# An attention and SwiGLU decode block on one core: the last gate's weights loaded with the other modulation weights, w2 in four pieces, the last K and V in fewer transfers

## The chip, the cores and the metric

One core of a Trainium2 chip runs the kernel. The metric is the device time of one execution in microseconds; three runs of the kernel before gave 242.71, 242.87 and 242.71, median 242.71 us. A profiled execution, from which all rows below come, took 242.85 us.

## What is computed

A decode step of a transformer block for a batch of B = 4 tokens, D = 512, in float32. The vector `c` (4 x 512) goes through silu and `w_mod` (512 x 3072) and gives six modulations: sa, ca, ga for the attention half, sb, cb, gb for the feed-forward half.

```python
mod = (_silu(c) @ w_mod).reshape(c.shape[0], 6, 1, -1)
sa, ca, ga, sb, cb, gb = (mod[:, 0], mod[:, 1], mod[:, 2], mod[:, 3], mod[:, 4], mod[:, 5])
h = _layernorm(x, axis=-1) * (1 + ca) + sa
x = x + ga * _A_ref(h, A_k_cache, A_v_cache, A_wq, A_wo)
h = _layernorm(x, axis=-1) * (1 + cb) + sb
x = x + gb * _B_ref(h, B_w1, B_w3, B_w2)
return x
```

`_A_ref` is attention over the last 2048 cached positions, 32 query heads on 8 key-value heads, with the projections wq and wo. `_B_ref` is `(silu(h @ w1) * (h @ w3)) @ w2` with 1792 hidden columns.

## The kernel before

All weights and the used part of the caches are laid out on the host so that every load is one rectangle of 128 partitions. About 99 MB pass through SP's DMA queue, in the order in which `load` (L92 to L94) issues them.

**The attention.** The 8 key-value heads are taken in 4 pairs. A pair's even head lies in the buffer `KV[0]`, its odd head in `KV[1]`, 8192 columns of K and 8192 of V each (8 MB a head). `WP` holds wo of the pair in its first half and wq of the next pair in its second. PE runs the loop body `pair` (L331 to L358): `scores`, a transpose of the probabilities (`turn`), `values`, a transpose of the result, and for the pair's heads `proj_out` with wo into the bank `bA`. ACT does the exponentials and scalings, DVE maxima, sums and re-layouts. SP's loads wait for the matmuls that free a buffer (`x_done`, `a_done`, `qt_done`). POOL passes the landing of K and V of the odd head on to PE, as semaphores that PE counts down (L142 to L148).

**The last head.** wo of the last pair (2 MB), K (4 MB), the first three quarters of V (3 MB, `dva`) and the last quarter (1 MB, `dvb`) are four transfers (L118 to L121).

**The tail.** Behind the last head come `wm` (ga, sb, cb of w_mod, 3 MB), `f1` (w1 and a part of w3, 4 MB), `f2` (the rest of w3, 3 MB), `gw` (gb's part of w_mod, 1 MB, and the first 8 of 28 units of w2, 1 MB) and w2's other 20 units in five transfers that end at the units `W2_CUTS` names. A unit is 256 columns, 128 KB; each transfer has its own semaphore. The order in which PE takes them is written out by hand behind the loop ("post", from L391 on):

- the sum over the four row groups of the attention output (`a_sb`, then bM, L368), and silu(c) times `wm` in three column groups of PE (L395), which ACT copies out as ga, sb, cb (L402);
- x1 = x + ga * attention, its norm on DVE and ACT (`stats` L150, `rroot` L165), h turned to `h2T` (L421, L424);
- h times f1 in four column groups (L432 to L435), copied to `g_sb` and turned; h times f2 (L442 to L445), copied to `u_sb` and turned (L461, L464); silu of the gate times the up part, as `hidT` (L448 to L467);
- gb's product in four row blocks (L470 to L472), copied by ACT to `gb_sb` (L475) and later spread and copied again to `gbJ` (L498 to L500);
- w2: the first 16 units as eight wide matmuls of 512 columns into `bO` (L484 to L487); their sum over the row blocks is spread into `bX` by `spread` (L278) from `y_sb` (L496, L502). The other 12 units go straight into `bX` as matmuls of 64 columns, eight for two units (L488 to L492), over four column groups;
- y = x1 + gb * (h w2), with both in the same spread layout (L505, L507), and the store (L509).

A float32 matmul of the program stands as two records in the trace.

Of the kernel before, what the change touches and what calls it, by code (L numbers as in the profile page):

```python
# [11 lines left out]
P = 128  # L12
# [4 lines left out]
HEAD = 8  # L17

W2_CUTS = [0, 8, 16, 20, 24, 27, 28]
H = 64  # L20
PAIRS = G // 2
W2_AT = 8192
# [25 lines left out]
def block_kernel(nc, x_in, t0_in, t1_in, kv_in, w_in, wm_in, f1_in, f2_in, gw_in, w2_in, out):  # L48
# [15 lines left out]
    dx, dt0, dt1, dkv, dk, dva, dvb, dwo, dm, df1, df2 = sems("dx dt0 dt1 dkv dk dva dvb dwo dm df1 df2")  # L64
    dw = sems(" ".join(f"dw{i}" for i in range(len(W2_CUTS) - 1)))
    z_ok, q_ok, p_ok, k_ok, va_ok, vb_ok, pt_ok, o_ok, ot_ok = sems("z_ok q_ok p_ok k_ok va_ok vb_ok pt_ok o_ok ot_ok")
# [3 lines left out]
    KV = [sb("KV0", 16384), sb("KV1", 16384)]  # L70
    WP = sb("WP", 8192)
# [6 lines left out]
    q_sb, p_sb, o_sb, a_sb, y_sb, g_sb, u_sb, gb_sb = [sb(n, 512) for n in "q_sb p_sb o_sb a_sb y_sb g_sb u_sb gb_sb".split()]  # L78
# [3 lines left out]
    sa_sb, ga_sb, sb_sb, cb_sb = [sb(n, 512, B) for n in "sa_sb ga_sb sb_sb cb_sb".split()]  # L82
# [5 lines left out]
    zero = y_sb  # L88
# [8 lines left out]
    s.dma_start(WP[:, 4096:], t1_in).then_inc(dt1, 16)  # L97
# [4 lines left out]
    for p in range(PAIRS):  # L102
        if p == PAIRS - 1:
            break
        S.wait_ge(qt_done, 2 * p + 2)
        if p:
            S.wait_ge(a_done, 2 * p)
        if p < PAIRS - 2:
            load(WP, w_in[p], dwo)
        else:  # L110
            load(WP, w_in[p], dwo)
        S.wait_ge(x_done, 2 * p + 1)
        load(KV[0], kv_in[2 * p + 2], dkv)
        S.wait_ge(x_done, 2 * p + 2)
        if p < PAIRS - 2:
            load(KV[1], kv_in[2 * p + 3], dk)
    S.wait_ge(a_done, G - 2)
    load(WP[:, :4096], w_in[PAIRS - 1][:, :4096], dwo)  # L118
    load(KV[1][:, :8192], kv_in[G - 1][:, :8192], dk)
    load(KV[1][:, 8192:14336], kv_in[G - 1][:, 8192:14336], dva)  # L120
    load(KV[1][:, 14336:], kv_in[G - 1][:, 14336:], dvb)  # L121
    S.wait_ge(x_done, G - 1)
    load(KV[0][:, :6144], wm_in, dm)
    load(KV[0][:, 6144:14336], f1_in, df1)
    S.wait_ge(x_done, G)
    load(KV[1][:, :6144], f2_in, df2)
    load(KV[1][:, 6144:10240], gw_in, dw[0])
    for a, b, sem in zip(W2_CUTS[1:-1], W2_CUTS[2:], dw[1:]):
        load(KV[1][:, W2_AT + a * 256 : W2_AT + b * 256], w2_in[:, (a - 8) * 256 : (b - 8) * 256], sem)
# [12 lines left out]
    for p in range(PAIRS - 1):  # L142
        gp.wait_ge(dk, 16 * (p + 1))
        for sem in (k_ok, va_ok, vb_ok):
            gp.sem_inc(sem, 1)
    for d, sem, n in ((dk, k_ok, 16 * PAIRS), (dva, va_ok, 16), (dvb, vb_ok, 16)):
        gp.wait_ge(d, n)
        gp.sem_inc(sem, 1)  # L148
# [134 lines left out]
    def project(u):  # L283
        for k in range(4):
            at = 4096 + 2048 * u + 512 * k
            ins = mm(bQ[32 * k : 32 * k + B, :], hT[:, k * B : (k + 1) * B], WP[:, at : at + 512])
        ins.then_inc(q_done, 1)
# [16 lines left out]
    def proj_out(u):  # L304
        take(ot_ok)
        for r in range(R):
            at = 2048 * u + 512 * r
            ins = mm(bA[32 * r : 32 * r + B, :], oT[:, r * B : (r + 1) * B], WP[:, at : at + 512], False, True)
        ins.then_inc(a_done, 1)
# [22 lines left out]
    with nc.body("pair", parent=root, valid_engines=[ET.PE]):  # L332
        T.reg_add(reg, reg, 1)
        take(dkv, 16)
        take(z_ok)
        scores(KV[0])
        project(1)
        take(p_ok)
        turn(bP, p_sb, pp_done)
        take(q_ok)  # L340
        turn(bT, q_sb, qt_done)
        take(pt_ok)
        values(KV[0], {})
        take(o_ok)
        turn(bX, o_sb, x_done)
        take(k_ok)
        take(z_ok)
        scores(KV[1])
        take(p_ok)
        turn(bP, p_sb, pp_done)  # L350
        take(dwo, 16)
        proj_out(0)
        take(pt_ok)
        values(KV[1], {0: va_ok, 3: vb_ok})
        take(o_ok)
        turn(bX, o_sb, x_done)
        proj_out(1)
        T.br_lt(reg, PAIRS, on_true="query", on_false="leave")  # L358
# [37 lines left out]
    for k in range(4):  # L396
        for i in range(3):
            at = (3 * k + i) * 512
            ins = mm(bX[32 * i : 32 * i + B, :], sc[:, k * B : (k + 1) * B], KV[0][:, at : at + 512], k == 0, k == 3)
    ins.then_inc(pe, 1)  # L400
    A.wait((pe, 4))
    t_ga, t_sb, t_cb = [A.op(s.copy(dst, bX[32 * i : 32 * i + B, :])) for i, dst in enumerate((ga_sb, sb_sb, cb_sb))]  # L402
# [14 lines left out]
    t_x1J = A.op(s.copy(x1J, bS[:, :H]))  # L417

# [4 lines left out]
    V.wait((pe, 6))  # L423
# [8 lines left out]
    for k in range(4):  # L432
        for j in range(4):
            at = 6144 + k * 2048 + j * 512
            ins = mm(bQ[32 * j : 32 * j + B, :], h2T[:, k * B : (k + 1) * B], KV[0][:, at : at + 512], k == 0, k == 3)  # L435
    ins.then_inc(pe, 1)
    A.wait((pe, 7))
# [9 lines left out]
    A.wait((pe, 8))  # L447
# [12 lines left out]
    V.wait((pe, 9))  # L460
# [5 lines left out]
    V.wait((pe, 10))  # L466
    t_hid = V.op(v.tensor_mul(hv[:, :, :3], view(sT)[:, :, :3], view(bS)[:, :, :3, :B]))  # L467


    T.wait_ge(dw[0], 16)  # L470
    for k in range(4):
        ins = mm(bM[32 * k : 32 * k + B, :], sc[:, k * B : (k + 1) * B], KV[1][:, 6144 + 512 * k : 6144 + 512 * (k + 1)])  # L472
    ins.then_inc(pe, 1)
    A.wait((pe, 11))
    t_gb = A.op(s.copy(gb_sb, bM))  # L475
    T.wait_ge(V.sem, t_hid[1])
    for i in range(len(W2_CUTS) - 1):
        if i:
            T.wait_ge(dw[i], 16)
        for n in range(W2_CUTS[i], W2_CUTS[i + 1]):  # L480
            if n < 26 and n % 2:
                continue
            jj, c = CHUNKS[n // 2]
            if n < 2 * HEAD:  # L484
                at, k = W2_AT + n * 256, n // 2
                ins = mm(bO[32 * (k % 4) : 32 * (k % 4) + B, :], hv[:, c, jj, :], KV[1][:, at : at + 512], k < 4, k >= HEAD - 4)
                continue  # L487
            for j in range(4):  # L488
                for r in (n % 2,) if n >= 26 else (0, 1):
                    at = W2_AT + (n * 256 + j * H if n >= 26 else n * 256 + j * P + r * H)  # L490
                    w = half(hw[:, c, jj, :], r)
                    ins = mm(bX[32 * j : 32 * j + 32, :H], w, KV[1][:, at : at + H], False, n == 27)  # L492
        if i == 1:
            ins.then_inc(pe, 1)
            V.wait((pe, 12))
            t_y = V.op(v.tensor_copy(y_sb, bO))  # L496
            T.wait_ge(A.sem, t_gb[1])
            spread(bT, same, gb_sb)  # L498
            A.wait((pe, 13))
            t_gb = A.op(s.copy(gbJ, bT[:, :H]))  # L500
            T.wait_ge(V.sem, t_y[1])
            spread(bX, same, y_sb, True, False)  # L502
    ins.then_inc(pe, 1)
    V.wait((pe, 14), t_gb)
# [9 lines left out]
def _layout(i):  # L514
    import numpy as np

    def a(t):
        return np.ascontiguousarray(t)

    k = i["A_k_cache"][:, :, SK - W :, :].reshape(B, G, NT, 512, DH)  # L520
    v = i["A_v_cache"][:, :, SK - W :, :].reshape(B, G, NT, 4, P, DH)
    k = k.transpose(1, 4, 2, 0, 3).reshape(G, P, 8192)
    v = v.transpose(1, 4, 2, 0, 3, 5).reshape(G, P, 8192)
    wm = i["w_mod"].reshape(4, P, 6, 512).transpose(1, 0, 2, 3)
    c = i["c"].reshape(B, 4, P).transpose(2, 1, 0).reshape(P, 16)
    wq = i["A_wq"].reshape(4, P, G, 512).transpose(2, 1, 0, 3).reshape(G, P, 2048)
    wo = i["A_wo"].reshape(G, R, P, D).transpose(0, 2, 1, 3).reshape(G, P, 2048)
    pairs = [[wo[2 * p], wo[2 * p + 1]] + ([wq[2 * p + 2], wq[2 * p + 3]] if p < 3 else [wo[6], wo[7]]) for p in range(4)]
    w1 = i["B_w1"].reshape(4, P, FF).transpose(1, 0, 2)
    w3 = i["B_w3"].reshape(4, P, FF).transpose(1, 0, 2)  # L530
    w2 = i["B_w2"].reshape(14, P, D)
    w2 = np.stack([w2[4 * j + c_] for j, c_ in CHUNKS], 1)
    w2[:, 13] = w2[:, 13].reshape(P, 4, 2, H).transpose(0, 2, 1, 3).reshape(P, D)
    w2 = w2.reshape(P, 14 * D)
    return {
        "x_in": a(i["A_x"].reshape(B, D)),
        "t0_in": np.concatenate([c, wm[:, :, 1::-1].reshape(P, 4096)], 1),
        "t1_in": np.concatenate([wq[0], wq[1]], 1),
        "kv_in": np.concatenate([k, v], 2),
        "w_in": np.stack([np.concatenate(p, 1) for p in pairs]),  # L540
        "wm_in": a(wm[:, :, 2:5]).reshape(P, 6144),
        "f1_in": np.concatenate([w1, w3[:, :, 1536:]], 2).reshape(P, 8192),
        "f2_in": a(w3[:, :, :1536]).reshape(P, 6144),
        "gw_in": np.concatenate([a(wm[:, :, 5]).reshape(P, 2048), w2[:, : 4 * D]], 1),
        "w2_in": a(w2[:, 4 * D :]),
    }
# [22 lines left out]
```

## Time and profile before

| | us |
|---|---|
| median of three runs | 242.71 |
| profiled execution, whole | 242.85 |
| its span, first to last instruction | 241.5 |
| DMA queue of SP: share of 16 engines' span | 95.6% (99.13 MB) |
| PE busy (matmuls) | 135.7 (56%) |
| DVE busy | 38.5 (16%) |
| ACT busy | 24.2 (10%) |

The span is the program's own time; 1.35 us of the profiled execution lie around it. A busy PE is no PE at its peak, since matmuls are pipelined and their ends are modelled; PEclk is the granted share of TensorE's clock, 1.00 for 2.4 GHz and 0.50 for 1.2 GHz. The landing of a DMA is its issue time plus the time to landing. Where a view merges several instructions, it gives the first one's start and the stretch to the end of the last one.

### The profile page before, as it was taken

Reading aid. Unit: us, or ns where it says so; the run is one execution under the profiler, and the core shown is the slowest. Engines: PE = TensorE matmul, PEld = TensorE weight load, DVE = VectorE, ACT = ScalarE, POOL = GpSimd, SP = SyncE. Lnnn points to the kernel's source line nnn. Section 1 sums busy time; section 2 is a strip of 40 time slices with the busy share of each in tenths; the row PEclk is TensorE's granted clock in tenths of the full one; section 3 lists DMA queues with packets and bytes.
Section 4 is the critical chain, followed back from the end, with each engine's and each line's share of the span. In section 5 each row is a group of like instructions: output and inputs, shape, how many; then the busy total and the mean of one; then the engine's idle time right before and its main releaser. Section 6 shows DMA issues by size and latency. Waiting matters only on the chain. (4 is left out here: it accounts for less than half of the span.)

```text
span 241.5 us, 2424 instructions
## 1 busy us (share of the span) xinstructions
PE 135.7 (56%) x1020; PEld 39.1 (16%) x1020; DVE 38.5 (16%) x126; ACT 24.2 (10%) x51; POOL 2.3 (1%) x15
## 2 busy tenths in 40 slices
PE   3004547818773378176613871757228767674885
PEld 0000121301221012012100120112001222111213
DVE  3003202201200022012000220220002222115121
ACT  2002101100110021001200021011000201122100
POOL 3000000000000000000000000000000000000000
PEclk9999958976589599679965699779957997995899
DMA  7998989899989898999898989998989999999992
GB/s 272 446 501 358 510 361 499 369 423 429 516 358 510 358 510 360 429 434 505 369 499 369 499 369 423 434 510 369 499 347 440 436 406 444 452 431 396 431 400 105
DMA packets 3756, 101.30 MB, mean 419 GB/s; under 512 B 548, under 2 KB 676, under 8 KB 1064
## 3 DMA queue, kind: packets, MB, share of 16 engines
q1 hardware_dynamic: 3600, 99.13, 95.6%
q10 hardware_dynamic: 152, 2.11, 2.1%
q8 instruction: 3, 0.05, 0.1%
q14 instruction: 1, 0.01, 0.0%
HBM read 101.20 MB, written 0.03 MB: 419 GB/s over the span
## 5 line engine op out<-in xcount | busy, mean ns | idle before, releaser
L257 PE MATMUL bS<-KV,Z 128*16 128x512 f32 x256 | 42.7, 827 | 41.1 <-PEq L273 41.1
L257 PE MATMUL bO<-KV,pT 128*16 128x512 f32 x256 | 32.9, 658 | 0.5
L257 PEld LDWEIGHTS bS<-KV,Z 128*16 128x16 f32 x256 | 9.2, 123 | 69.1 <-issue 69.1
L220 DVE TENSOR_REDUCE MX<-bS 128x1 f32<-128x512 f32 x8 | 5.5, 692 | 82.2 <-PE bS L257 82.2
L382 ACT ACTIVATE p_sb<-bS,NB 128x512 f32<-128x512 f32 x8 | 5.5, 687 | 103.7 <-ACTq L373 103.7
L291 PE MATMUL bP<-ident,p_sb 128*128 128x128 f32 x32 | 5.5, 298 | 17.3 <-PEq L273 17.3
L257 PE MATMUL bM<-KV,sc 128*4 128x512 f32 x24 | 5.9, 711 | 16.0 <-DVE sc L190 16.0
L257 PE MATMUL bA<-WP,oT 128*4 128x512 f32 x64 | 10.4, 731 | 4.0 <-PEq L273 4.0
L257 PEld LDWEIGHTS bO<-KV,pT 128*16 128x16 f32 x256 | 8.4, 106 | 23.5 <-issue 23.5
L387 ACT ACTIVATE o_sb<-bO,LB 128x512 f32<-128x512 f32 x8 | 5.5, 687 | 48.9 <-ACTq L373 48.9
L291 PE MATMUL bX<-ident,o_sb 128*128 128x128 f32 x32 | 5.0, 280 | 7.8 <-PEq L273 7.8
L246 DVE TENSOR_REDUCE oT<-bX 128x16 f32<-128x64 f32 x8 | 1.8, 224 | 43.7 <-PE bX L291 43.7
L257 PE MATMUL bQ<-WP,hT 128*4 128x512 f32 x64 | 8.3, 592 | 0.6 <-DVE hT L199 0.6
L291 PEld LDWEIGHTS bP<-ident,p_sb 128*128 128x128 f32 x32 | 3.6, 150 | 24.4 <-issue 24.4
L291 PE MATMUL bT<-ident,q_sb 128*128 128x128 f32 x32 | 5.4, 296 | 3.6 <-PEq L273 3.6
L291 PEld LDWEIGHTS bX<-ident,o_sb 128*128 128x128 f32 x32 | 3.4, 140 | 15.0 <-issue 15.0
L229 DVE COPY pT<-bP 128x256 f32<-128x256 f32 x8 | 3.4, 425 | 14.1 <-PE bP L291 14.1
L257 PE MATMUL bQ<-KV,h2T 128*4 128x512 f32 x32 | 5.4, 842 | 0.3 <-DVE h2T L424 0.3
L291 PEld LDWEIGHTS bT<-ident,q_sb 128*128 128x128 f32 x32 | 3.6, 147 | 7.5 <-issue 7.2
L257 PE MATMUL bX<-KV,sc 128*4 128x512 f32 x24 | 4.4, 592 | 0.0
L257 PEld LDWEIGHTS bM<-KV,sc 128*4 128x4 f32 x24 | 0.9, 96 | 20.9 <-DVE sc L190 17.6
L204 DVE TENSOR_REDUCE Z<-bT 128x16 f32<-128x64 f32 x8 | 1.8, 225 | 14.5 <-PE bT L291 14.2
(104 smaller groups left out, 69.2 us busy)
## 6 DMA issues: line engine op xcount, KB each, us to landing
WP<-w_in SPq DMA_DIRECT2D x3, 4096.0 KB, 19.7
KV<-kv_in SPq DMA_DIRECT2D x1, 4096.0 KB, 24.0
KV<-f_in SPq DMA_DIRECT2D x1, 4096.0 KB, 25.6
KV<-kv_in SPq DMA_DIRECT2D x1, 3072.0 KB, 30.8
KV<-wm_in SPq DMA_DIRECT2D x1, 3072.0 KB, 16.3
KV<-f_in SPq DMA_DIRECT2D x1, 3072.0 KB, 18.8
KV<-t_in SPq DMA_DIRECT2D x1, 2056.0 KB, 12.3
WP<-t_in ACTq DMA_DIRECT2D x1, 2048.0 KB, 12.5
```

Source lines behind the costliest of these rows:

```text
L204: v.tensor_reduce(Z.rearrange("p (b i) -> p b i", b=B)[:, :, 12 : 12 + R], bT.rearrange("p (r k i) -> p i r k", r=R, k=4)[:, :B], axis=AX. ...
L220: t = V.op(v.reduce_max(MX[:, 0:1], bS, axis=AX.X))
L229: v.tensor_copy(pT.rearrange("p (t b c r) -> p c b t r", t=NT, b=B, c=4), bP.rearrange("p (c b i) -> p c b i", c=4, b=B)[:, :, :, :16].rea ...
L246: V.op(v.tensor_reduce(oT.rearrange("p (r b) -> p r b", r=R), diag, axis=AX.X, op=ALU.add), ot_ok)
L257: return T.matmul(o, lhsT, rhs, start=start, stop=stop, skip_group_check=True)
L291: ins = T.transpose(dst[:, c * P : (c + 1) * P], src[:, c * P : (c + 1) * P], ident)
L382: A.op(s.activation(p_sb, bS, AF.Exp, bias=NB[:, 0:1], accum_out=SM[:, 0:1]), p_ok)
L387: A.op(s.mul(o_sb, bO, LB[:, 0:1]), o_ok)
```

## The change

Three things change, and the buffers with them.

1. **gb's weights** move from the transfer `gw` behind f2 into `wm`, which has now four of w_mod's parts (4 MB) and goes into the first half of `KV[0]`, with f1 in the second half. gb's product is a fourth column group of the modulation matmuls; ACT copies it behind cb, and its spread into the layout of the result stands right behind x1's.
2. **w2** comes in four transfers of 16, 8, 3 and 1 units behind f2, and all 28 units run as matmuls of 64 columns straight into `bX`. The wide matmuls, `y_sb` and its spread are gone.
3. **The last head**: WP and `KV[1]` become two parts of one buffer, `WK`, with wq in WP's first half and wo in its second, beside K. So wo of the last pair and the last K are one transfer (6 MB) on the semaphore of K; POOL, when it lands, also releases PE's wait for wo. V of the last head is one transfer (4 MB).

```diff
-W2_CUTS = [0, 8, 16, 20, 24, 27, 28]
+W2_CUTS = [0, 16, 24, 27, 28]
...
-    KV = [sb("KV0", 16384), sb("KV1", 16384)]
-    WP = sb("WP", 8192)
+    WK = sb("WK", 8192 + 16384)
+    KV = [sb("KV0", 16384), WK[:, 8192:]]
+    WP = WK[:, :8192]
...
     S.wait_ge(a_done, G - 2)
-    load(WP[:, :4096], w_in[PAIRS - 1][:, :4096], dwo)
-    load(KV[1][:, :8192], kv_in[G - 1][:, :8192], dk)
-    load(KV[1][:, 8192:14336], kv_in[G - 1][:, 8192:14336], dva)
-    load(KV[1][:, 14336:], kv_in[G - 1][:, 14336:], dvb)
+    load(WK[:, 4096:16384], wk_in, dk)
+    load(KV[1][:, 8192:], v_in, dv)
     S.wait_ge(x_done, G - 1)
-    load(KV[0][:, :6144], wm_in, dm)
-    load(KV[0][:, 6144:14336], f1_in, df1)
+    load(KV[0][:, :8192], wm_in, dm)
+    load(KV[0][:, 8192:], f1_in, df1)
     S.wait_ge(x_done, G)
     load(KV[1][:, :6144], f2_in, df2)
-    load(KV[1][:, 6144:10240], gw_in, dw[0])
-    for a, b, sem in zip(W2_CUTS[1:-1], W2_CUTS[2:], dw[1:]):
-        load(KV[1][:, W2_AT + a * 256 : W2_AT + b * 256], w2_in[:, (a - 8) * 256 : (b - 8) * 256], sem)
+    for a, b, sem in zip(W2_CUTS[:-1], W2_CUTS[1:], dw):
+        load(KV[1][:, W2_AT + a * 256 : W2_AT + b * 256], w2_in[:, a * 256 : b * 256], sem)
...
-        for sem in (k_ok, va_ok, vb_ok):
+        for sem in (k_ok, v_ok):
             gp.sem_inc(sem, 1)
-    for d, sem, n in ((dk, k_ok, 16 * PAIRS), (dva, va_ok, 16), (dvb, vb_ok, 16)):
-        gp.wait_ge(d, n)
-        gp.sem_inc(sem, 1)
+    gp.wait_ge(dk, 16 * PAIRS)
+    gp.sem_inc(k_ok, 1)
+    gp.sem_inc(dwo, 16)
+    gp.wait_ge(dv, 16)
+    gp.sem_inc(v_ok, 1)
...
-        values(KV[1], {0: va_ok, 3: vb_ok})
+        values(KV[1], {0: v_ok})
...
-        for i in range(3):
-            at = (3 * k + i) * 512
+        for i in range(4):
+            at = (4 * k + i) * 512
...
-    t_ga, t_sb, t_cb = [A.op(s.copy(dst, bX[32 * i : 32 * i + B, :])) for i, dst in enumerate((ga_sb, sb_sb, cb_sb))]
+    t_ga, t_sb, t_cb, t_gb = [A.op(s.copy(dst, bX[32 * i : 32 * i + B, :])) for i, dst in enumerate((ga_sb, sb_sb, cb_sb, gb_sb))]
...
+    T.wait_ge(A.sem, t_gb[1])
+    spread(bO, same[:B], gb_sb)
+    A.wait((pe, 6))
+    t_gbJ = A.op(s.copy(gbJ, bO[:, :H]))
...
-    T.wait_ge(dw[0], 16)
-    for k in range(4):
-        ins = mm(bM[32 * k : 32 * k + B, :], sc[:, k * B : (k + 1) * B], KV[1][:, 6144 + 512 * k : 6144 + 512 * (k + 1)])
-    ins.then_inc(pe, 1)
-    A.wait((pe, 11))
-    t_gb = A.op(s.copy(gb_sb, bM))
     T.wait_ge(V.sem, t_hid[1])
     for i in range(len(W2_CUTS) - 1):
-        if i:
-            T.wait_ge(dw[i], 16)
+        T.wait_ge(dw[i], 16)
...
-            if n < 2 * HEAD:
-                at, k = W2_AT + n * 256, n // 2
-                ins = mm(bO[32 * (k % 4) : 32 * (k % 4) + B, :], hv[:, c, jj, :], KV[1][:, at : at + 512], k < 4, k >= HEAD - 4)
-                continue
...
-                    ins = mm(bX[32 * j : 32 * j + 32, :H], w, KV[1][:, at : at + H], False, n == 27)
-        if i == 1:
-            ins.then_inc(pe, 1)
-            V.wait((pe, 12))
-            t_y = V.op(v.tensor_copy(y_sb, bO))
-            T.wait_ge(A.sem, t_gb[1])
-            spread(bT, same, gb_sb)
-            A.wait((pe, 13))
-            t_gb = A.op(s.copy(gbJ, bT[:, :H]))
-            T.wait_ge(V.sem, t_y[1])
-            spread(bX, same, y_sb, True, False)
+                    ins = mm(bX[32 * j : 32 * j + 32, :H], w, KV[1][:, at : at + H], n == 0 and r == 0, n == 27)
```

The order of PE's instructions in the tail, from the product with f2 on, with the semaphores they wait for (`dw0` and on are the landings of w2's transfers in turn, `dve` and `act` those engines). Before:

```order
L257 MATMUL bA<-KV,h2T 4x512 [waits df2]
L464 MATMUL bS<-ident,u_sb 128x96 [waits dve]
L257 MATMUL bM<-KV,sc 4x512 [waits dw0]
L257 MATMUL bO<-KV,hidT 4x512 [waits dve]
L257 MATMUL bO<-KV,hidT 4x512 [waits dw1]
L257 MATMUL bT<-gb_sb,same 32x64 [waits act]
L257 MATMUL bX<-y_sb,same 32x64 [waits dve]
L257 MATMUL bX<-KV,hidT 32x64 [waits dw2]
L257 MATMUL bX<-KV,hidT 32x64 [waits dw3]
L257 MATMUL bX<-KV,hidT 32x64 [waits dw4]
L257 MATMUL bX<-KV,hidT 32x64 [waits dw5]
```

And in the changed kernel:

```order
L253 MATMUL bA<-WK,h2T 4x512 [waits df2]
L464 MATMUL bS<-ident,u_sb 128x96 [waits dve]
L253 MATMUL bX<-WK,hidT 32x64 [waits dw0,dve]
L253 MATMUL bX<-WK,hidT 32x64 x63
L253 MATMUL bX<-WK,hidT 32x64 [waits dw1]
L253 MATMUL bX<-WK,hidT 32x64 x31
L253 MATMUL bX<-WK,hidT 32x64 [waits dw2]
L253 MATMUL bX<-WK,hidT 32x64 x11
L253 MATMUL bX<-WK,hidT 32x64 [waits dw3]
```

gb's product and spread and the wide part of w2 have left this stretch; behind `hidT` stand 112 small matmuls (64, 32, 12 and 4) with four waits.

The order of SP's loads from the last pair's wo on, before:

```order
L94 DMA WP<-w_in 128x4096 [waits a_done,x_done]
L94 DMA KV<-kv_in 128x8192
L94 DMA KV<-kv_in 128x6144
L94 DMA KV<-kv_in 128x2048
L94 DMA KV<-wm_in 128x6144 [waits x_done]
L94 DMA KV<-f_in 128x8192
L94 DMA KV<-f_in 128x6144 [waits x_done]
L94 DMA KV<-gw_in 128x4096
L94 DMA KV<-w_in 128x2048
L94 DMA KV<-w_in 128x1024 x2
L94 DMA KV<-w_in 128x768
L94 DMA KV<-w_in 128x256
```

And in the changed kernel:

```order
L94 DMA WK<-wk_in 128x12288 [waits a_done,x_done]
L94 DMA WK<-v_in 128x8192
L94 DMA KV<-wm_in 128x8192 [waits x_done]
L94 DMA KV<-f_in 128x8192
L94 DMA WK<-f_in 128x6144 [waits x_done]
L94 DMA WK<-w_in 128x4096
L94 DMA WK<-w_in 128x2048
L94 DMA WK<-w_in 128x768
L94 DMA WK<-w_in 128x256
```

Thirteen transfers have become nine; the waits stand at the same places.

## Rows read from the trace of the kernel before

**Rows 1.** The page: DMA busy tenths in 40 slices; shares of the chain that ended last.
```profile
DMA  7998989899989898999898989998989999999992
...
DMA 11%; SPq 1%; PE 1%; DVE 0%; issue 0%
```
**Rows 2.** The chain that ended last, in order: start us, us, what.
```profile
211.26 27.45 DMA KV<-w_in
...
238.75 0.73 PE bX L257 x32
```
**Rows 3.** DMA issues: out<-in, engine, operation, count, size, median us to landing.
```profile
KV<-f_in SPq DMA_DIRECT2D x1, 4096.0 KB, 25.6
...
KV<-wm_in SPq DMA_DIRECT2D x1, 3072.0 KB, 16.3
KV<-f_in SPq DMA_DIRECT2D x1, 3072.0 KB, 18.8
...
KV<-kv_in SPq DMA_DIRECT2D x1, 1024.0 KB, 32.8
...
KV<-w_in SPq DMA_DIRECT2D x1, 1024.0 KB, 25.4
...
KV<-w_in SPq DMA_DIRECT2D x1, 384.0 KB, 27.4
KV<-w_in SPq DMA_DIRECT2D x1, 128.0 KB, 27.3
```
**Rows 4.** Timeline of SP from 165 us: start us, us, what, count.
```profile
169.74 1.38 SPq L94 DMA_DIRECT2D KV<-kv_in  x3
194.51 0.33 SPq L94 DMA_DIRECT2D KV<-wm_in  x1
194.88 14.44 SPq L94 DMA_DIRECT2D KV<-f_in  x2
...
209.84 2.33 SPq L94 DMA_DIRECT2D KV<-w_in  x5
```
**Rows 5.** DMA queues in 54.5:60, 234.8:235.4, 235:239: packets, MB, share of 16 engines.
```profile
q1 hardware_dynamic: 72, 2.36, 99.3%
...
q1 hardware_dynamic: 67, 0.23, 96.3%
...
q8 instruction: 1, 0.02, 1.7%
```
**Rows 6.** Two stretches: length, busy us (count) by engine, PEclk, DMA share, GB/s.
```profile
221.50:225.25 3.75, 3.74 (x20) 0.70 (x24) 0.00 (x0) 0.00 (x0) 0.00 (x0) 0.50 0.99 424
225.25:227.00 1.75, 1.71 (x16) 0.20 (x8) 0.00 (x0) 0.00 (x0) 0.00 (x0) 1.00 1.01 431
```
**Rows 7.** Timeline of the tail: start us, us, engine, line, what, count [idle before].
```profile
202.70 4.65 PE L257 MATMUL bO<-KV,pT 128*16 128x512 f32 x32
...
211.22 0.59 PE L257 MATMUL bM<-a_sb,same 128*4 128x512 f32 x1 [0.81 <-DVE a_sb L394]
...
215.75 0.57 ACT L402 COPY ga_sb<-bX 4x512 f32<-4x512 f32 x1 [7.56 <-PE bX L257]
...
216.95 0.58 ACT L402 COPY cb_sb<-bX 4x512 f32<-4x512 f32 x1
...
218.03 0.72 ACT L156 ACTIVATE sq<-x,st 4x512 f32<-4x512 f32 x1 [0.51 <-DVE st L154]
...
221.51 5.45 PE L257 MATMUL bQ<-KV,h2T 128*4 128x512 f32 x32 [0.27 <-DVE h2T L424]
...
228.26 3.61 PE L257 MATMUL bA<-KV,h2T 128*4 128x512 f32 x24
...
233.58 0.11 PEld L257 LDWEIGHTS bO<-KV,hidT 128*4 128x4 f32 x4 [0.32 <-DVE hidT L467]
...
237.37 1.15 PE L257 MATMUL bX<-KV,hidT 128*32 128x64 f32 x64
238.75 0.72 PE L257 MATMUL bX<-KV,hidT 128*32 128x64 f32 x32 [0.24 <-DMA KV<-w_in]
```

## Prediction: the gate's weights moved forward, w2 in four pieces, the last K and V in fewer transfers

> **What bounds the kernel now.** I read four views in this order: the slices of the page, the chain that ended last, the DMA issues with their times to landing, and the timeline of the last 40 us. The slices show the DMA engines busy from the second slice to the last but one, 8 or 9 tenths and never less [rows 1]. The chain that ended last has hardly any compute in it: one DMA wait of 27.45 us, from the issue of the 384 KB piece of w2 at 211.26 to its landing at 238.71, then 0.73 us of matmuls, two small DVE operations and the store [rows 1, 2]. So the kernel is one long stream of 99 MB, and the end is "the last bytes land, plus about 2.8 us". The reader should see in the issues that the stream is never short of work: the last nine transfers wait 16 to 27 us between issue and landing [rows 3], because SP has issued the whole tail by 212.17 [rows 4]. What SP's issues cost (0.33 to 0.48 us each) is therefore free. Only two things move the end: how long the engines take over the same bytes, and whether PE, when the last pieces land, still has older work to do.
>
> **Bytes and transfers.** The bytes are the same: 1,024 KB of gate weights move from behind f2 to in front of f1, nothing is added. The number of transfers falls by four: wo and K in one, V in one, and six tail transfers (gw and five of w2) become four. Price of a transfer: while only 32 KB packets run, 72 packets take 99.3% of 16 engines over 5.5 us, 1.21 us each, or 27 bytes per ns; near the end 67 packets carry 0.23 MB in 96.3% of 16 engines over 0.6 us, 9.24 us, where the bytes alone would be 8.5 us [rows 5]. The rest is 0.7 us over 67 packets, 8 to 14 ns each with the rounding of the megabytes. A transfer has 128 rows on 16 engines, 8 packets on each, and a word for its semaphore: 9 times 8 ns is 0.07 us, at the upper end 0.13 us. Four of them are **0.3 us** (ends: 0, if packets hide it, and 0.5 us). I take the low price, since the 32 KB packets carry a share of it in their own rate. The Trainium skill (DMA: Bandwidth & Descriptors, "Anatomy of one DMA — SWDGE (gpsimd) path") gives each DMA a fixed cost of about 2.0 us; by that the four would be worth 8 us. The trace disagrees for queued transfers: the 384 KB and the 128 KB piece land 0.3 us apart [rows 2 to 4], so I give that rule under 0.01.
>
> **Where the pieces land then.** Before: wm 194.51 + 16.3 = 210.8, f1 194.88 + 25.6 = 220.5, f2 208.99 + 18.8 = 227.8, w2's first MB 209.84 + 25.4 = 235.2, the last piece 211.74 + 27.3 = 239.0 [rows 3, 4]. f1's 4,096 KB took 9.67 us, so 1,024 KB take 2.42 us. After: two transfers fewer in front (-0.14) and one MB more for wm, f1 and f2: **wm 213.1, f1 222.8, f2 230.1**. The w2 pieces: [0,16) at 235.0, [16,24) at 237.4, [24,27) at 238.4, the last at 238.8.
>
> **V in one transfer.** V is whole at 203.5 now [rows 3, 4], 203.4 then. Before, the values matmuls started at 202.70 on the first three quarters [rows 7]; now they start at 203.4, 0.7 us late, and so does what hangs on them: the fold of a_sb, from 211.22 to 211.9 [rows 7], and SP's issue of f2, from 208.99 to 209.7. The first ends before wm lands at 213.1; the second is 20 us ahead of its turn. Cost nothing, cover 1.2 us. K with wo lands when K did; wo is read after K's scores: nothing. On POOL two waits replace three; PE's take of wo is released by POOL after K, early enough.
>
> **The modulation stage.** The fourth column group rides along with three: 24 matmuls over three groups take 3.61 us [rows 7], eight rounds, and 32 over four groups have eight rounds too. So wm's product runs 213.1 to 216.7. From the first copy (ga) at 215.75 to f1's matmuls at 221.51 were 5.76 us; the new copy of gb (0.58 us as cb's) stands on ACT ahead of the squares, which had 0.50 us of room between 217.53 and 218.03 [rows 7]: +0.1. h is ready at about 222.6, f1 lands at 222.8: nothing. The spread of gb (16 matmuls, under 0.5 us) falls into PE's idle time while DVE and ACT do the norm.
>
> **From f1 to the end.** f1's matmuls to f2's took 6.75 us (221.51 to 228.26) [rows 7]: 222.8 + 6.75 = 229.6, so f2's now wait for f2 at 230.1. From there to w2's first weight load were 5.32 us (228.26 to 233.58): w2 starts at S = 235.4, when [0,16) is there. Gone from the tail are gb's product, its copies and spread and the wide part of w2 with its own spread, all that stood between 233.58 and 237.37. In their place w2 runs wholly as small matmuls: 112 in the program, 224 in the records. 64 took 1.15 us, 32 took 0.72 us [rows 7]; without the last one's 0.22 us that is 14.5 and 15.6 ns each. At 15 ns, 224 are 3.36 us: 235.4 + 3.36 + 0.22 = 239.0. By the pieces: from [16,24) at 237.4, 64 take 0.96 us to 238.4, just when [24,27) lands; 32 more take 0.72: **239.2 against 239.47 before, -0.28 us**. So the DMA stream still ends last, but only by 0.2 us; S = 235.6 is the point from which PE decides, S = 235.9 that from which nothing is gained.
>
> **The clock decides S.** f1's matmuls began at a granted clock of 0.50 (1.2 GHz), after PE had been almost idle, and it rose to 1.00 (2.4 GHz) at 225.25, after 3.74 us of matmuls without a pause [rows 6]; they took 5.45 us [rows 7]. If it rises as late into them as before, S stays. If all stay at the low level, they take 5.45 + 1.71 = 7.2 us, f2's start at 231.3 and S = 236.6. Rows cannot tell where between; the middle costs some 0.2 us of the 0.28. I forecast **-0.1 us**: the profiled execution's 242.85 becomes 242.75, and against the median of 242.71, which lies 0.14 lower, **242.6 us: no change that can be measured**. The bound for that is 0.2%, 0.49 us.
>
> **Rivals.** *PE ends last* (slower). Place: f1's matmuls at the low clock throughout, S = 236.6: end at 236.6 + 3.36 + 0.22 = 240.2, +0.7, **243.3 us**. If the low level covers f2's eight rounds as well (3.61 becomes some 7.0), +3.4 more. For it: these matmuls start from idle, and 1.3 us later than before. Against: PE has had a fuller stage just ahead. The same wait would come from the burst itself: 18 ns each (1.15 us over 64) add 0.7 us. Also PE's program grows by 96 records of w2 and a code fetch (the instruction queue's packet in the tail [rows 5], 1.7% of 16 engines over 4 us, 1.1 us) that now falls into the burst could hold it up by so much. Chance of slower 0.23. The Trainium skill (TensorE: Matmul & The Clock Gate, "Back-to-back issue gap") lets no matmul follow another in under 25 ns; by that the burst is 5.6 us and the time 244.5. The rows above, 14.5 ns, disagree for this shape over four column groups, so I give it 0.02 within the 0.23.
>
> *Transfers cost more than I take* (faster). At 0.13 us each, four are 0.5 us, and f2 is earlier too: 238.97, **242.2 us**. For it: small pieces. Against: the low price fits the 32 KB packets best, and PE's route must be early as well. Chance 0.11.
>
> *It does nothing*: the lists of instructions do show 20 loads on SP where 24 were, so this is only the case in which packets hide the price: 242.7 to 242.9, inside the forecast. Chance of no change 0.66.
>
> **Numbers.** The likeliest case holds 242.3 to 243.0. The range reaches into both rivals: 242.2 (0.5 us off) to 243.4 (S = 236.6 and some), which leaves out two in ten, mostly a longer low clock above.
>
> **What would show it.** Right: transfers of w2 landing 0.3 us earlier, f2's matmuls waiting for their DMA, w2's 224 records without long gaps, a chain that still ends with a DMA. Wrong: a chain that runs back through PE and DVE to f2 (PE's route); f1's records all at 0.50; a gap in w2's matmuls that no landing ends; landings later than 238.8.

## The result and the profile after

The changed kernel takes **244.09 us** (median, 243.94 to 244.23) against 242.80 us for the kernel before in the same comparison (242.71 to 243.17): ratio 1.005, 95% interval 1.0037 to 1.0063. It is 1.3 us slower. The forecast was 242.6 us, no measurable change, with a range of 242.2 to 243.4: wrong.

The page of the changed kernel, its slices and the shares of the chain that ended last:

```profile
DMA  7999999989998989898989898989899999999990
...
PE 8%; ACT 2%; DVE 1%; issue 1%
```

Against [rows 1] the DMA engines are as busy as before, but the last slice is empty (0 where 2 stood), and the chain that ended last holds no DMA any more. The stream of loads is over before the kernel is. The issues and SP's timeline tell when:

```profile
WK<-wk_in SPq DMA_DIRECT2D x1, 6144.0 KB, 24.3
WK<-v_in SPq DMA_DIRECT2D x1, 4096.0 KB, 33.7
KV<-wm_in SPq DMA_DIRECT2D x1, 4096.0 KB, 18.9
KV<-f_in SPq DMA_DIRECT2D x1, 4096.0 KB, 28.3
WK<-f_in SPq DMA_DIRECT2D x1, 3072.0 KB, 19.4
WK<-w_in SPq DMA_DIRECT2D x1, 2048.0 KB, 23.9
WK<-w_in SPq DMA_DIRECT2D x1, 1024.0 KB, 25.9
WK<-w_in SPq DMA_DIRECT2D x1, 384.0 KB, 26.4
WK<-w_in SPq DMA_DIRECT2D x1, 128.0 KB, 26.2
```

```profile
193.95 0.33 SPq L94 DMA_DIRECT2D KV<-wm_in  x1
194.32 0.43 SPq L94 DMA_DIRECT2D KV<-f_in  x1
210.53 0.33 SPq L94 DMA_DIRECT2D WK<-f_in  x1
210.90 1.86 SPq L94 DMA_DIRECT2D WK<-w_in  x4
```

Issue plus time to landing: f2 at 229.9, w2's four pieces at 234.8, 237.3, 238.3 and 238.5 (the last three were issued at 211.38, 211.85 and 212.33: four issues in 1.86 us, with 0.04 us between two). The last landing was at 239.0 before [rows 3, 4], so the stream ends 0.5 us earlier. The time went to PE. Its pieces of the chain that ended last, and its timeline of the end, with the idle time in front in brackets:

```profile
235.53 2.04 PE bX L253 x124
237.57 1.63 issue
239.20 1.64 PE bX L253 x94
```

```profile
223.07 5.91 PE L253 MATMUL bQ<-KV,h2T 128*4 128x512 f32 x32 [0.27 <-DVE h2T L424]
...
230.28 3.61 PE L253 MATMUL bA<-WK,h2T 128*4 128x512 f32 x24
...
235.53 2.04 PE L253 MATMUL bX<-WK,hidT 128*32 128x64 f32 x127 [0.30 <-DVE hidT L467]
239.20 1.62 PE L253 MATMUL bX<-WK,hidT 128*32 128x64 f32 x97 [1.63 <-issue]
240.86 0.23 DVE L483 TENSOR_TENSOR yt<-bX,gbJ 128x64 f32<-128x64 f32 x1 [5.38 <-PE bX L253]
```

The reader should see three things. The burst of w2 (its 112 matmuls, 224 records, meant to run without a pause) begins at 235.53, where the forecast had 235.4, and runs at the pace that [rows 7] gave: 127 records in 2.04 us. Then PE stands for 1.63 us. And the place is odd: the first piece of w2 is 64 matmuls, 128 records, so PE stops one record *ahead* of the end of that piece, in the middle of a matmul's two records, with the weights of that piece there since 234.8. No wait of the program stands at that place ("issue": nothing that the profile shows), and the next piece, [16,24), had landed at 237.3. In the same stretch, 236 to 238, the instruction queue (q8 in the list of DMA queues) moves one packet:

```profile
q8 instruction: 1, 0.02, 3.2%
```

That is 3.2% of 16 engines over 2 us, 1.02 us for one block of code; there is none from 232 to 236.7, and there is one from 236.72 on. So the theory that I tested was **code fetch**: PE has used up the instructions that it holds, at the border of a block of its program, and stands until the next block is there. The rivals were that the landing of [16,24) reaches PE late, and that the clock or the shape of the small matmuls costs the time.

### The profile page after: what moved, and what is told of

It is laid out like the page before. It is cut to its first block, busy times and chain, and to the rows that moved or that the text cites. A ratio compares the mean times of both kernels' runs of the same rounds, so it can differ in the third digit from the quotient of the medians.

```text
span 242.9 us, 2604 instructions
## 1 busy us (share of the span) xinstructions
PE 139.5 (57%) x1116; PEld 40.7 (17%) x1116; DVE 37.8 (16%) x125; ACT 24.0 (10%) x51; POOL 2.3 (1%) x15
## 5 line engine op out<-in xcount | busy, mean ns | idle before, releaser
L253 PE MATMUL bS<-KV,Z 128*16 128x512 f32 x128 | 22.7, 873 | 23.7 <-PEq L269 23.7
L253 PE MATMUL bS<-WK,Z 128*16 128x512 f32 x128 | 20.7, 806 | 13.7 <-PEq L269 13.7
L253 PE MATMUL bO<-WK,pT 128*16 128x512 f32 x128 | 19.7, 771 | 0.7 <-PEq L269 0.7
L253 PE MATMUL bM<-WK,sc 128*4 128x512 f32 x16 | 6.1, 932 | 16.1 <-DVE sc L186 16.1
L253 PE MATMUL bO<-KV,pT 128*16 128x512 f32 x128 | 14.5, 593 | 0.5
L253 PE MATMUL bA<-WK,oT 128*4 128x512 f32 x64 | 10.7, 747 | 3.9 <-PEq L269 3.9
L253 PE MATMUL bQ<-WK,hT 128*4 128x512 f32 x64 | 9.2, 648 | 0.6 <-DVE hT L195 0.6
L253 PEld LDWEIGHTS bS<-WK,Z 128*16 128x16 f32 x128 | 4.5, 120 | 26.9 <-issue 26.9
L253 PEld LDWEIGHTS bO<-WK,pT 128*16 128x16 f32 x128 | 4.8, 122 | 17.4 <-issue 17.4
L253 PEld LDWEIGHTS bO<-KV,pT 128*16 128x16 f32 x128 | 3.8, 96 | 8.5 <-issue 8.5
```

The lines of the kernel that those rows point to most:

```text
L253: return T.matmul(o, lhsT, rhs, start=start, stop=stop, skip_group_check=True)
```

## Experiments

All were timed against the kernel before on the same chip; its medians there were 242.77 to 242.84 us.

**Shift the program by 26 records.** 13 matmuls that nothing needs, in PE's idle time behind the spread of gb, change neither the burst's instructions, nor its waits, nor the transfers:

```diff
     spread(bO, same[:B], gb_sb)
+    for i in range(13):
+        mm(bM[32 * (i % 4) : 32 * (i % 4) + 32, :H], half(same[:B], 0), gb_sb[:, :H])
```

> The changed kernel with 13 more matmuls of 64 columns (26 records, 52 instructions) behind the spread of gb, where PE stands idle; nothing reads what they write. Theory, code fetch: PE takes its program in blocks of 256 instructions; it reaches a block border at the last records of w2's first piece, at 237.35, while the fetch of the next block began only at the border before, just ahead of the burst, and so PE stands until 239.20. 26 records more in front put the border at about the 101st record of the burst, the border before it at the start of f2's matmuls (230.3, five us earlier), and the next one behind the end: no gap, w2 runs through by 239.0, the end follows the last landings: span about 241.3, time 242.5 us (242.3 to 242.8), 1.6 us less than the changed kernel although PE does more. Rival, the landing of the piece [16,24) is seen late: neither the wait nor the transfer changed, so the gap stays in front of the same piece at the same time and the time stays at 244.1. Rival, clock or shape of the small matmuls: as the changed kernel, 244.1 or a little more.

Measured: 242.47 us (242.32 to 242.77, 11 runs) against 242.77, ratio 0.9988, interval 0.9979 to 0.9996. The burst of this kernel, in PE's timeline:

```profile
229.98 3.61 PE L253 MATMUL bA<-WK,h2T 128*4 128x512 f32 x24 [0.91 <-DMA WK<-f_in]
234.39 0.55 PE L466 MATMUL bS<-ident,u_sb 96*128 96x96 f32 x4 [0.80 <-DVE u_sb L463]
235.24 3.81 PE L253 MATMUL bX<-WK,hidT 128*32 128x64 f32 x224 [0.30 <-DVE hidT L469]
```

All 224 records stand in one piece, with no gap, and the chain that ended last goes back to a landing of w2:

```profile
210.28 27.04 DMA WK<-w_in
237.31 0.04 issue
237.36 1.71 PE bX L253 x93
```

The code's packet is there ten us earlier, between 226 and 228:

```profile
q8 instruction: 1, 0.02, 3.2%
```

More work on PE and 1.62 us less time: late landing and the matmuls' shape are out, since both are the same here ([16,24) lands at 237.3 in both). The gap of 1.63 us is about the whole of that difference. The burst also began 0.3 us earlier, at 235.24: f1's matmuls took 4.93 us here and 5.91 in the changed kernel, at a granted clock of 0.67 and 0.50 from 221 to 227.7. That this removed the gap is ruled out by the kernel with eight added matmuls below: its profile has 5.06 us and 0.65 there, its burst begins at 235.16, and it stops. This version beats both kernels, the one before by 0.30 us.

**Shift it by 64 records.** The same loop with 32.

> The same with 32 instead of 13 added matmuls (64 records). Theory, code fetch: the border in the burst moves 64 records forward, to about the 63rd, which is covered (its fetch began in f2's stage), but the next border, 127 records on, falls at about the 190th record. Its fetch begins when PE passes the 63rd at 236.4 and needs the 3.7 us that it needed in the changed kernel, so PE stands from about 238.3 to 240.1 with some 34 records left: end of matmuls 240.8, time 244.0 us (243.6 to 244.2), the gap at record 185 to 195. Rival, more work in front helps by keeping PE's clock high or by some other way that grows with the padding: as fast as with 13 or faster, 242.5, and no gap. Rival, late landing: gap at the 127th record as in the changed kernel, 244.1.

Measured: 243.57 us (243.42 to 244.27), ratio 1.0041 (1.0028 to 1.0054). The gap is back, elsewhere:

```profile
235.27 3.22 PE L253 MATMUL bX<-WK,hidT 128*32 128x64 f32 x191 [0.30 <-DVE hidT L469]
239.31 0.68 PE L253 MATMUL bX<-WK,hidT 128*32 128x64 f32 x33 [0.82 <-issue]
```

127 less 64 is 63, where the theory has a border and PE passes without a stop; the stop is behind record 191, which is 128 records on, as forecast (185 to 195). A record of the burst is a weight load and a matmul, so 128 records are 256 instructions. The Trainium skill (Runtime: NRT & Kernel Launch, "Instruction fetch mechanics") says that instructions are refilled in blocks of 16 KiB, 256 instructions. The trace agrees on the size: 0.02 MB a packet and borders 128 records apart. The same section calls the cost of crossing a block "mostly hidden"; that differs here: it is 0.82 us in this kernel and 1.63 us in the changed one. The gap was shorter than I took, 0.82 us, since PE goes on at 239.31 and not at 240.1.

**Shift it by 2, 6 and 16 records** (1, 3 and 8 added matmuls).

> The changed kernel with one added matmul behind the spread of gb (2 records, 4 instructions). Theory, code fetch: in the changed kernel the block border lies within an instruction or two of the first of w2's matmuls, behind the turn of u, where PE waits for DVE. Four instructions more put it into that turn, so that PE's sequencer may pass it before it waits for u's copy: then the fetch begins two us earlier and the gap is gone or under 0.5 us: 242.5 to 243.2, with some executions that still stand (the runs spread over 1 us or more). Rival, the gap needs the large shift of 26 records, since what counts is the time of f2's stage: 244.1 as the changed kernel. Rival, late landing or clock: 244.1.

> The same with three added matmuls (6 records, 12 instructions). Theory, code fetch: the border lies ahead of the turn of u, at the last of f2's matmuls, and is passed by 233.5 in every execution; the code is there by 237, when PE reaches record 121 of the burst at 237.1 to 237.2: no gap or under 0.3 us, 242.5 us (242.3 to 242.9), runs as close together as with 13. Rival, as above: 244.1.

> The changed kernel with 8 added matmuls (16 records, 32 instructions), between the 3 that did not help and the 13 that did. The border lies at record 111 of the burst, the one before it in the middle of f2's matmuls. If the sequencer's position alone decided, the fetch would begin by 232 and there would be no gap (242.5 us). If the fetch in the tail always waits until engines run dry at 236.5, the gap stands in front of record 112, from 237.1 to 239.1: 244.1 us.

Measured: with one 244.06 us (243.99 to 244.21, ratio 1.0054, 1.0041 to 1.0067), with three 244.17 us (243.89 to 244.35, ratio 1.0052, 1.004 to 1.0065), with eight 243.26 us, ten runs from 242.28 to 244.42 (ratio 1.0017, 0.9994 to 1.0041). The place moved as the theory says, by two records for each added matmul: the burst breaks behind record 125, 121 and 111. The lines with one, with three and with eight:

```profile
236.07 2.04 PE L253 MATMUL bX<-WK,hidT 128*32 128x64 f32 x125 [0.30 <-DVE hidT L469]
238.91 1.67 PE L253 MATMUL bX<-WK,hidT 128*32 128x64 f32 x99 [0.80 <-issue]
```

```profile
235.30 2.01 PE L253 MATMUL bX<-WK,hidT 128*32 128x64 f32 x121 [0.30 <-DVE hidT L469]
239.18 1.76 PE L253 MATMUL bX<-WK,hidT 128*32 128x64 f32 x103 [1.87 <-issue]
```

```profile
235.16 1.81 PE L253 MATMUL bX<-WK,hidT 128*32 128x64 f32 x111 [0.30 <-DVE hidT L469]
238.50 1.85 PE L253 MATMUL bX<-WK,hidT 128*32 128x64 f32 x113 [1.53 <-issue]
```

But the time did not follow: I had expected that one might do and that three suffice, since their border lies in f2's matmuls. The packet still came between 236 and 237 with one, three and eight (236.49, 236.54 and 236.07). So the place is given by the program, and the moment of the fetch by something else. In all seven profiles with a stop (these three, the changed kernel, 32 added and the two below with 2.60 and 3.60 us) PE goes on 2.4 to 2.6 us after its packet starts: it waits for that packet. With eight, five of ten runs lie under 242.7 and five over 243.8: the times fall into two groups with 1.16 us between them, as if the gap were either there or not. Only one of the ten, with the gap, has a profile.

**What the fetch waits for.** Two kernels with the burst of the changed one. One leaves out the four loads of w2 and PE's waits for them (the matmuls read what lies in the buffer), the other adds 2 MB behind w2:

```diff
-    for a, b, sem in zip(W2_CUTS[:-1], W2_CUTS[1:], dw):
-        load(KV[1][:, W2_AT + a * 256 : W2_AT + b * 256], w2_in[:, a * 256 : b * 256], sem)
...
-        T.wait_ge(dw[i], 16)
```

```diff
+    S.wait_ge(pe, 4)
+    load(KV[0][:, :4096], w2_in[:, :4096], dex)
...
+    S.wait_ge(dex, 16)
```

> The changed kernel without the four loads of w2 and without PE's waits for them; the 112 matmuls run on what lies in the buffer. Left out: 3.5 MB of loads, so that the DMA engines have no data to move from 229.9 on. It asks why the fetch of the code comes as late as 236.5 to 236.9 in so many variants, with three and with no added matmuls. Theory, the fetch waits at its DMA engine behind w2's data: with empty engines the packet runs by 234, PE has the code before it needs it, no gap in the burst; matmuls from 235.5 to 239.0, time 242.3 us or less. Rival, the fetch begins only when PE's sequencer passes the border and takes its 3 us whatever the engines do: packet at 236 to 237, gap of 1 us or more in front of record 128 as in the changed kernel, time 243.2 to 244.1.

> The changed kernel with one more load of 2 MB behind w2's, into the part of the buffer where the modulation weights were, which nothing reads; the store waits for it. Read from the gap, not from the time (the added load alone ends at 243.4, so the time is 246 us or more). Theory, the fetch waits behind all data of its engine: the packet starts at 241 or later, PE goes on at 243 or later. Theory, the fetch waits behind the small packets of the last pieces alone or for nothing of the kind: packet near 236.7, PE goes on at 239.2 to 239.7.

Measured without the loads: 242.40 us (ten runs, nine of them 242.14 to 242.70, one 243.97), ratio 0.9986 (0.9971 to 1.0001). Its burst and its packet, the latter in 231 to 232, the only packet of any queue from 230 to 232:

```profile
235.30 3.41 PE L251 MATMUL bX<-WK,hidT 128*32 128x64 f32 x224 [0.30 <-DVE hidT L465]
```

```profile
q8 instruction: 1, 0.02, 8.4%
```

Measured with 2 MB more: 247.21 us, one run, which says nothing by itself since the store waits for the added load. Its burst and its packet, the latter in 238.5 to 239:

```profile
235.76 2.04 PE L255 MATMUL bX<-WK,hidT 128*32 128x64 f32 x127 [0.30 <-DVE hidT L469]
241.40 2.44 PE L255 MATMUL bX<-WK,hidT 128*32 128x64 f32 x97 [3.60 <-issue]
```

```profile
q8 instruction: 1, 0.02, 12.7%
```

The packet starts at 231.06 when the engines have no data, at 236.72 with w2 in the queues, at 238.90 with 2 MB more. PE is not stopped in the first kernel, stopped for 1.63 us in the second, and for 3.60 us at the same record in the third. So **these runs speak for a fetch of the code that waits behind data on the DMA engines**, and what makes the gap is both: the block border in the burst, and the stream that the fetch has to get through. It does not wait for all of it: 2 MB more are 4.9 us at the rate of [rows 5], the packet came 2.2 us later, between the two places that I had forecast (236.7, and 241 or later).

Three things limit this. The kernel without the loads also lacks PE's four waits, and one of its ten runs, 243.97 without a profile, is as long as one with a stop. The kernel with 2 MB more has one run. And with V in two transfers (below) a packet came at 233.7 with all of w2 in the queues. The Trainium skill (DMA: Bandwidth & Descriptors, "Queues, rings and completion order") has each engine take turns between its queues packet by packet, a packet there being typically 9 to 17 descriptors, where the packets of this case's profile are single rows. An engine's share of w2's first piece is 8 rows of 16 KB, an estimated 4.9 us at the 27 bytes per ns worked out from [rows 5]. The packet came 5.7 us earlier without w2 and 2.2 us later with more, so a turn of that length is neither confirmed nor refuted here.

**w2's part of the change alone.** The kernel before, with all of w2 as small matmuls:

```diff
-            if n < 2 * HEAD:
-                at, k = W2_AT + n * 256, n // 2
-                ins = mm(bO[32 * (k % 4) : 32 * (k % 4) + B, :], hv[:, c, jj, :], KV[1][:, at : at + 512], k < 4, k >= HEAD - 4)
-                continue
...
-            T.wait_ge(V.sem, t_y[1])
-            spread(bX, same, y_sb, True, False)
```

> The kernel before with one part of the change alone: all of w2 as matmuls of 64 columns straight into the result's bank, no wide matmuls, no copy and spread of their sum; loads and gb's product as before. Theory, code fetch: the same number of instructions as in the changed kernel's burst, but the burst is spread over 5 us by the landings (from 233.6 on), so that a border and the one before it lie more than 2.5 us apart; PE may stand about 1 us near the piece [16,20), and is back before the piece that lands at 238.7. Time as before, 242.8 us (242.5 to 243.1). Rival, small matmuls cost more than the wide ones in themselves: slower by 0.5 us or more, 243.3 or above, without one long gap.

Measured: 244.67 us (243.67 to 245.20), ratio 1.007 (1.0051 to 1.0089). A miss in size. The gap stands where the count puts it: behind 143 records (128 of w2 and 15 of the spread of gb), 16 later than in the changed kernel, since 16 records fewer of gb's product and spread and of the modulation stand in front. But in the profiled run, 245.14 us, it lasts 2.60 us, not one:

```profile
236.19 0.19 PE bT L257 x13
236.39 2.60 issue
238.99 0.27 PE bT L257
```

This part alone costs at least as much as the whole change (1.0051 to 1.0089 against 1.0037 to 1.0063). The pieces of w2 spread the burst over five us, and that did not help, since here too the packet comes between 236 and 237, at 236.40.

**Everything but w2's part.** The changed kernel with the wide matmuls, `y_sb` and its spread, and w2 in six pieces.

> The changed kernel with w2's part undone: pieces of 8, 8, 4, 4, 3 and 1 units, the first 16 units as wide matmuls, their copy and spread as before; gb's weights forward and the merged last K and V stay. Theory: no gap, since the tail has 128 records fewer, but f2 lands 2.3 us later than before, so the wide matmuls run 235.5 to 237.3, the copy ends at 238.1, the spread at 238.5, 64 records by 239.4 and the last 32 by 239.9: 0.4 us behind before, 243.2 us (242.9 to 243.5). Rival, the loss lies in the later f2 or the merged V: 244 or more. Rival, all of it is w2's matmuls and the rest is the gain that I took for the transfers: 242.5.

Measured: 243.63 us (243.34 to 245.99, 12 runs), ratio 1.0044 (1.0027 to 1.0062); 0.1 us over the range that I gave. No gap by code in the profile; the wide matmuls, the copy and the spread are a serial chain behind f2, which lands 2 us later than before:

```profile
235.75 1.90 PE L255 MATMUL bM<-WK,hidT 128*4 128x512 f32 x16 [0.30 <-DVE hidT L469]
238.47 0.45 PE L255 MATMUL bX<-y_sb,same 128*32 128x64 f32 x16 [0.81 <-DVE y_sb L490]
238.72 1.60 PE L255 MATMUL bX<-WK,hidT 128*32 128x64 f32 x96
```

So with gb's weights in front of f2, the small matmuls are the better form of w2 when the code is there in time: 242.47 us with 13 added against 243.63 here.

**V in two transfers again**, alone and with 13 added matmuls:

```diff
-    load(KV[1][:, 8192:], v_in, dv)
+    load(KV[1][:, 8192:14336], v_in[:, :6144], dv)
+    load(KV[1][:, 14336:], v_in[:, 6144:], dvb)
...
-        values(KV[1], {0: v_ok})
+        values(KV[1], {0: v_ok, 3: vb_ok})
```

> The changed kernel with one part undone: V of the last head again in three quarters and one quarter, with PE waiting for each. Theory: the values matmuls start at 202.7 instead of 203.35, the modulation stage again waits for its weights and not for the fold, f2's matmuls start at their landing, 229.9 or 230.0, instead of 230.28; the burst starts 0.3 us earlier, the border before it is passed as much earlier and the gap stays 1.6 to 1.9 us: time 243.8 us (243.6 to 244.0). Rival, the merged V costs the whole loss: 242.7. Rival, it costs nothing: 244.1.

> 13 added matmuls and V of the last head in two transfers. Theory: without the gap the end hangs on the last landings of w2, which one transfer more moves by 0.07 us later; PE starts the burst up to 0.3 us earlier, which gains nothing there: 242.5 us as with 13 added alone (242.3 to 242.7). Rival, the burst still sets the end: 0.2 us faster than with 13 alone.

Measured alone: 243.95 us, six runs from 242.41 to 244.90; the ratio of 1.0057 (1.0044 to 1.0071) fits the five without the shortest, which average 244.17. The median lies in the forecast, the spread does not: one run has no gap. That is the profiled one; its packet starts between 233 and 234, and all 224 records stand in one piece:

```profile
235.62 3.41 PE L256 MATMUL bX<-WK,hidT 128*32 128x64 f32 x224 [0.30 <-DVE hidT L470]
```

Nor did the burst start 0.3 us earlier, as I had said it would: f1's matmuls began at their landing but took 6.40 us. The edit puts one wait more into PE's loop, by which the border would move by one instruction; without a stop in the profile that is not shown. With 13 added: 242.43 us (ten of eleven runs 242.27 to 242.66, one 243.84), ratio 0.9991 (0.9981 to 1.0002), as with 13 alone. V's transfers are worth nothing here that these runs can show.

## Why the prediction was wrong

**Bytes and transfers: the size fits, the cause is not shown.** I took 0.28 to 0.3 us, with ends 0 and 0.5; the last landing came 0.5 us earlier in the changed kernel, and the version without the gap is 0.30 us faster than the kernel before. But between profiles with the same loads the last landing moves by 0.2 to 0.3 us: 238.5 in the changed kernel and 238.8 with one added matmul, 239.0 in the kernel before and 238.8 with its w2 in small matmuls. No run isolates the price of a transfer. The rule of 2.0 us that the prediction takes from the Trainium skill stands there for DMAs on the gpsimd path, and these loads are SP's; nothing of its 8 us is seen.

**Landings: right.** Forecast and measured: wm 213.1 and 212.9, f1 222.8 and 222.6, f2 230.1 and 229.9, w2 235.0, 237.4, 238.4, 238.8 and 234.8, 237.3, 238.3, 238.5.

**V and the modulation stage: nearly right, with less room than I wrote.** V was there at 203.2 and the values matmuls started at 203.35, but they took 5.54 us instead of 4.65 [rows 7] (granted clock 0.50 from 203.4 to 206.4, 0.77 before), so the fold of a_sb began at 212.76 and not at 211.9; of a cover of 1.2 us 0.1 was left. h came later than I took: f1's matmuls began at 223.07, 0.5 us behind their landing, and f2's at 230.28, 0.35 us behind theirs. So the sign "f2's matmuls waiting for their DMA" did not come, and "a chain that runs back through PE and DVE to f2" did; with 13 added matmuls both waited for their landings.

**S, the start of the burst, and the clock: right.** f1's matmuls stayed at 0.50 nearly to their end (5.91 us, between the 5.45 and the 7.2 that I gave). Two stretches, in the columns of [rows 6]:

```profile
220.91:227.74 6.83, 5.26 (x28) 1.35 (x32) 1.27 (x4) 0.38 (x3) 0.00 (x0) 0.50 1.00 428
227.74:242.00 14.26, 9.64 (x268) 4.95 (x260) 2.47 (x8) 0.81 (x2) 0.00 (x0) 1.00 0.62 255
```

S was 235.53, against 235.4, and the burst ran wholly at 1.00. S stayed under the 235.6 from which, by my sum, PE decides. (One sum is 0.1 us off: 238.4 and 0.72 are 239.1, not 239.2; nothing hangs on it.)

**The step that failed** is "at 15 ns, 224 are 3.36 us". The pace was right: without the loads 224 records took 3.41 us, 14.2 ns each without the last one's 0.22. The rule of 25 ns that the prediction takes from the Trainium skill does not hold in the records of this shape. What was wrong is that the sum let the burst run without a break. I had the break among the rivals, in half a sentence, as a code fetch "that now falls into the burst", at 1.1 us, and held it as unlikely as the rest of that rival; its sign, "a gap in w2's matmuls that no landing ends", came. Two numbers were missed. The price is not the packet's 1.1 us: from the packet's start to PE's going on were 2.5 us in the changed kernel (from 236.72 to 239.20) and 2.4 us in the one with 64 records (from 236.93 to 239.31). And the chance was to be worked out: the kernel before shows code packets while PE runs the tail (at 214.4 and 236.8), and 224 small records in place of 96 are more than one block. So a border had to fall into a burst that uses up a block in 1.9 us, less than the 2.4 us from packet to going on; whether PE stops there hangs on how early the packet comes. With 1.63 us of stop and the 0.30 us that the version without it gains, the sum is +1.3 us, which is what was measured.

**Still open** is how long a fetch waits and by what rule. It did not wait for all data, 13 added matmuls brought it to 226.96 although data filled the engines then too, and at the edge (eight added, or one wait more) the times say that it is early in some executions and late in others. Its starts bunch: where all of w2 and no more is in the queues, the first packet behind 222 us lies at 226.0 to 227.0 in three profiles (13, 32, and 13 with V in two), at 236.0 to 237.0 in seven (the kernel before among them), and only once between, at 233.7. That would fit a code queue that seldom gets a turn beside the data, but no run tests it. That PE stood for its code was shown; that data holds the fetch is what the two kernels with other loads speak for; how it gets past was not shown.

## What to carry to other kernels

Straight-line code on PE had to be loaded here like data: count a burst's instructions against the block (256 of them, 128 records here) and ask whether the block behind its border can arrive before PE gets there, with the DMA engines full. A gap that sits at a fixed count of instructions, in the middle of a piece of work, with all operands there, was code in each kernel here; moving the program by some instructions is the test for it. It can also be the cure (13 idle matmuls: -1.62 us), but not one to rely on: three did nothing, with eight half of the runs were slow, and 32 brought a stop back. When a change replaces few wide matmuls by many small ones, price the instructions as well as the matmul time.

## What the runs showed that I had not expected

The fetch of PE's code came later the more data the DMA engines had: with the same matmuls PE did not stop in the profile without w2's loads, stopped for 1.63 us with them and for 3.60 us with 2 MB more behind them (one run). And once the packet has moved (1.02 us), PE stands for about another 1.5 us before it goes on (from 237.74 to 239.20).
